# Attention and feed-forward kernel: q of five batches turned by DMA, in f16 halves, in place of TensorE transposes

## The chip, the core and the metric

The kernel runs on one core of a Trainium2 chip. The metric is the device time in microseconds. Before the change the median of three runs is 868.02 us (866.51 to 870.14).

A core has a matrix engine (TensorE, PE in the profile, its weight loads PEld), three elementwise engines (VectorE or DVE, ScalarE or ACT, GpSimd or POOL) and a queue engine (SyncE, SP) that here only starts DMAs. Each runs its own instruction queue in order and waits on semaphores for the others.

## The reference

Linear attention with 8 batches, 8 heads, 576 positions and 64 features a head, then a feed-forward layer over all 4608 tokens:

```python
q_s = softmax(q, axis=features);  k_s = softmax(k, axis=positions)
kv  = einsum('bhsd,bhse->bhde', k_s, v)          # one 64 x 64 matrix a head
x   = einsum('bhsd,bhde->bhse', q_s, kv)         # to [4608, 512]
h   = x @ w_in                                   # 512 -> 2048
out = (h * erf(softplus(h))) @ w_out             # 2048 -> 512
```

All inputs and the output are f32.

## The kernel before, in words

**Numbers.** Most f32 products are made from f16 halves: a value a is split into hi = f16(a) and lo = f16(a - hi), and a product is three f16 products (hi hi, hi lo, lo hi). A split is a copy on ACT and a subtraction on DVE. Only batches 0 and 1 and the first block of the feed-forward layer stay in f32 (`E32 = 2`).

**Feed-forward.** The tokens of two batches (a pair, 1152 tokens) are three blocks of 384. A block goes through four groups of 512 hidden features, so the kernel has 48 steps n. In step n PE makes the first product of step n in four parts m n.0 to m n.3 (function `mm1`, L905, with seven half-size products in place of eight, in product banks X, Y and Z, which ACT and DVE empty at L917 to L932), and the second product of step n - 2 in three parts M.0 to M.2 (`mm2`, L1029). Between them lie softplus and erf on ACT (L337), the multiplication (L984) and the split (L997, L1001) on DVE. Each bank of X, Y, Z exists once: PE refills it only when its last content is copied out.

**Attention.** `attention(b)` makes x for one batch. It is a generator; its stages are worked in between the parts of the feed-forward steps. A share is written for each stage (`SHARES`), and after each part of the second product `pace` takes stages until their summed shares reach the goal for that point in the program. The stages of a batch are: maximum of k over positions (`k_max`); q minus its maximum (`q_sub`); exponentials; first kv products, first half of q normalized (`q_norm`, L454 to L460); second kv products, loads of the next k and v; the kv matrix normalized and split (`kv_norm`, `kv_split`, L588, L589); second half of q normalized, and in odd batches the tail of both batches of the pair. Half means four heads over the first 512 positions; a tail is the last 64 positions of a batch, and the tails of two batches share one tile.

Then x is made for four blocks c of two heads each: PE transposes four 128x128 squares of q (`q_cols`, L610) into a bank, ACT and DVE split the bank into two f16 halves (`q_evac`, L603, L604), and, a stage later, three f16 products with kv give x (`x_mm`, L625), which ACT copies out (L436). In odd batches the tail comes ahead of the four blocks (transposes L684, the same evacuation, products into the tile xt). Behind the transposes of the second and fourth blocks stand the loads of the next batch's q (`load_q`), four DMAs each on SP.

**Order.** What the code issues is placed on each engine's queue by data and priority when the program is built; an instruction can stand earlier than its place in the code when its inputs are there early. The queues then run in that order. SP's queue carries the loads of q, k and v and the stores of results.

**Buffers.** The tiles tagged `qT` rotate over two places of 512 columns: kmax, k2, kvf and the evacuated q. The tile `raw`, 2048 f32 columns, takes raw weights and one decoded weight block at the start, which is read for the last time in step 6.

Of the kernel before, what the change touches and what calls it, by code (L numbers as in the profile page):

```python
# [8 lines left out]
F16 = mybir.dt.float16  # L9
# [44 lines left out]
def attn_moe_kernel(  # L54
# [29 lines left out]
    ch = ctx.enter_context(tc.tile_pool(name="ch", bufs=1))  # L84
    at = ctx.enter_context(tc.tile_pool(name="at", bufs=2))
    xp = ctx.enter_context(tc.tile_pool(name="xp", bufs=2))
    rp = ctx.enter_context(tc.tile_pool(name="rp", bufs=1))
    psh = ctx.enter_context(tc.tile_pool(name="psh", bufs=1, space=PSUM))
    pso = ctx.enter_context(tc.tile_pool(name="pso", bufs=1, space=PSUM))
    psa = ctx.enter_context(tc.tile_pool(name="psa", bufs=2, space=PSUM))  # L90
# [6 lines left out]
    vbuf = cp.tile([P, 4, TM, D + 1], F32, name="vbuf")  # L97
    nc.gpsimd.memset(vbuf[:, :, :, D:], 1.0)
    vtail = cp.tile([P, H, D + 1], F32, name="vtail")

    kvbd = []
    for i in range(2):
# [51 lines left out]
    def wload():  # L154


        i = nxt[0]
        while i < NPC * NJ and slots:
            w = slots.pop(0)
            if i >= NPC * (NJ - 1 if w is None else NJ if w < 2 else w - 2):  # L160
                continue
            if w == -1:
                w, other = None, "x7"
            else:
                other = None
            which, g = wjobs[i // NPC]
            a = i % NPC
            if which == "in":
                src = w_in[a * 2 * P:(a + 1) * 2 * P, 2 * g * 512:2 * (g + 1) * 512]
            else:  # L170
                src = w_out[(4 * g + 2 * a) * P:(4 * g + 2 * a + 2) * P, :]
            if other:

                raws[i] = xp.tile([P, 2, 1024], I32, tag=other, name=f"raw_{i}")
            elif w is None:
                raws[i] = rp.tile([P, 2, 1024], I32, tag="raw", bufs=1, name=f"raw_{i}")
            else:
                raws[i] = WT[w][:, :4096].bitcast(I32).rearrange("p (a n) -> p a n", a=2)
            held[i] = -1 if other else w

            eng = nc.sync if i < LOADS.count("w") else nc.gpsimd
            eng.dma_start(raws[i], src.rearrange("(a p) n -> p a n", p=P))
            nxt[0] += 1
            return

    def wdecode(i, part=None):


        jn, a = divmod(i, NPC)
        if jn not in stg:  # L190
            if jn + 2 < NJ:
                stg[jn] = WT[jn + 2][:, :4096].bitcast(F32)
            elif jn == NJ - 2:
                stg[jn] = xp.tile([P, 2048], F32, tag="x7", name=f"sg_{jn}")
            else:
                stg[jn] = rp.tile([P, 2048], F32, tag="raw", bufs=1, name=f"sg_{jn}")
        d = stg[jn][:, a * 1024:(a + 1) * 1024].bitcast(I32)
        if part is None:
            r = raws[i].rearrange("p a n -> p (a n)").rearrange("p (n two) -> p n two", two=2)
        else:  # L200
            r = raws[i][:, :, 512 * part:512 * part + 512].rearrange(
                "p a (n two) -> p a n two", two=2
            )
            d = d.rearrange("p (a n) -> p a n", a=2)[:, :, 256 * part:256 * part + 256]
        lo, hi = r[..., 0], r[..., 1]
        nc.vector.tensor_scalar(
            d, hi, 5, 2, op0=ALU.logical_shift_left, op1=ALU.logical_shift_right,
        )
        nc.vector.scalar_tensor_tensor(
            d, lo, 29, d, op0=ALU.logical_shift_right, op1=ALU.bitwise_or  # L210
        )
        nc.vector.scalar_tensor_tensor(
            d, hi, -(2**30), d, op0=ALU.bitwise_and, op1=ALU.bitwise_or
        )
        if part == 0:
            return
        raws.pop(i)
        h = held.pop(i)
        if h != -1:
            slots.append(h)  # L220
        wload()
# [262 lines left out]

    def k_max(b, ks, kt):

        kmax = at.tile([P, H, D], F32, tag="qT", name=f"kmax_{b}")
        k2 = at.tile([P, 2, 4, D], F32, tag="qT", name=f"k2_{b}")
        for hf in range(2):
            nc.vector.tensor_tensor(k2, ks[hf][:, 0:2], ks[hf][:, 2:4], op=ALU.max)  # L490
            nc.vector.tensor_tensor(
                kmax[:, hf * 4:hf * 4 + 4, :], k2[:, 0], k2[:, 1], op=ALU.max
            )
        nc.vector.tensor_tensor(kmax[kt[1]], kmax[kt[1]], kt[0], op=ALU.max)
        return kmax
# [44 lines left out]

    E32 = 2
    kv32 = [t.rearrange("p h c e -> p (h c e)").bitcast(F32) for t in kvbd]
    kv32 = [t.rearrange("p (c e) -> p c e", c=NC4) for t in kv32]

    def kv_norm(b, hf, bk):
        if b >= E32:
            if hf == 0:
                bat[b]["kvf"] = at.tile([P, NC4, D], F32, tag="qT", name=f"kvf_{b}")  # L550
            kvf = bat[b]["kvf"]
        bkv = bk[:, :2 * W].rearrange("p (c w) -> p c w", c=2)
        rd = at.tile([P, 2, 1], F32, tag="rd", bufs=1, name=f"rd_{b}_{hf}")
        nc.vector.tensor_scalar_add(rd, bkv[:, :, D:], 1e-9)
        nc.vector.reciprocal(rd, rd)
        cs = slice(2 * hf, 2 * hf + 2)
        if b >= E32:
            nc.vector.tensor_tensor(
                kvf[:, cs, :], bkv[:, :, :D], rd.to_broadcast([P, 2, D]), op=ALU.mult
            )  # L560
            return
        for a in range(2):
            ps = slice(a * D, (a + 1) * D)
            nc.vector.tensor_tensor(
                kv32[b][ps, cs, ps], bkv[ps, :, :D], rd[ps].to_broadcast([D, 2, D]),
                op=ALU.mult,
            )
# [25 lines left out]
        if b > 1:  # L593
            nc.vector.tensor_scalar_mul(d["U"], w_u["in"], d["ux"])

    def q_evac(b, bk, name):

        if b < E32:
            qT = at.tile([P, SM], F32, tag="qT", name=name)
            nc.scalar.copy(qT, bk)  # L600
            return qT[:, None, :]
        qT = at.tile([P, 2, SM], F16, tag="qT", name=name)
        nc.scalar.copy(qT[:, 0], bk)  # L603
        nc.vector.tensor_tensor(qT[:, 1], bk, qT[:, 0], op=ALU.subtract)  # L604
        return qT
# [8 lines left out]

    def q_T(b, c, bk):
        q_cols(b, c, bk)
        return q_evac(b, bk, f"qTs_{b}_{c}")

    def x_mm(b, c, out_, qT):

# [15 lines left out]
    def attention(b):  # L636
# [26 lines left out]
        d["v"].append(load_half(v, "v", b, 1))  # L663
        q_norm(rows(qs[0]), 16, f"q_{b}_0", b)
        yield SHARES[5]
        kv_norm(b, 1, kv_mm(b, 1))
        if b + 1 < B:
            load_kv(b + 1)
# [2 lines left out]
        kv_split(b, mx)  # L671
        yield SHARES[7]
        q_norm(rows(qs[1]), 16, f"q_{b}_1", b)
        if j == 1:
            q_norm(even["qt"], H, f"qt_{p}", b)
        yield SHARES[8]
        for i in ((3 * p + 1, 3 * p + 2) if j else (3 * p, 3 * p + 1)):
            while not x_free(i):
                yield 0
        if j == 1:  # L680
            qt2 = hd(even["qt"])
            bk = bank(f"qTt_{p}")
            for c in range(NC4):
                nc.tensor.transpose(  # L684
                    bk[:, c * P:(c + 1) * P], qt2[:, c * P:(c + 1) * P], ident
                )
            qT = q_evac(b, bk, f"qTt_{p}")
            if b + 1 < B:
                even_next = bat[b + 1]
                even_next["qt"] = load_tail(q, "qt", p + 1)  # L690
            yield SHARES[9]
            bk = bank(f"xt_{p}")
            x = xblock(p * NBK + 1)
            bk3 = bk.rearrange("p (c s) -> p c s", c=NC4)
            for a in range(2):
                for c in range(NC4):
                    cs = slice(c * P + a * TAIL, c * P + (a + 1) * TAIL)
                    x_mm(2 * p + a, c, bk[:, cs], qT[:, :, cs])
            for a in range(2 if b < E32 else 1):
                w = TAIL if b < E32 else P  # L700
                o = SM - T + a * TAIL
                x_put(
                    bk3[:, :, a * TAIL:a * TAIL + w], x[:, :, o:o + w],
                    bat[a]["sx"] if b < E32 else None,
                )
            yield SHARES[10]
        for c in range(NC4):
            hf, c2 = divmod(c, 2)
            qT = q_T(b, c, bank(f"qT_{b}_{c}"))
            if c2 == 1 and b + 1 < B:  # L710
                load_q(b + 1, hf)
            yield SHARES[11]
            bk = bank(f"x_{b}_{c}")
            x_mm(b, c, bk, qT)
            x_split(b, c, bk)
            if c == NC4 - 1:
                d["xdone"] = True
            yield SHARES[12]
# [14 lines left out]
    def start():  # L733
# [61 lines left out]
        def tc_(c):  # L795
# [3 lines left out]
            if c < 3:  # L799
                bk = psh.tile([P, 512], F32, tag=f"p{'XYZ'[c]}", name=f"qT_0_{c}")  # L800
                qT = r["qT"][:, c]
            else:
                bk = pso.tile([P, 512], F32, tag="o2", name=f"qT_0_{c}")
                qT = at.tile([P, SM], F32, tag="qT", name=f"qTs_0_{c}")
            q_cols(0, c, bk)
            nc.scalar.copy(qT, bk)
            put(f"t{c}", qT[:, None, :])
# [373 lines left out]
```

## Time and profile before

| what | before |
|---|---|
| runs, median (lowest, highest) | 868.02 us (866.51, 870.14) |
| profiled execution: span | 865.1 us |
| profiled execution: its own time beside the span | not listed apart; the three runs are the times there are |
| PE, busy | 823.4 us, 95% |
| DVE, busy | 642.5 us, 74% |
| ACT, busy | 505.9 us, 58% |
| POOL, busy | 18.2 us, 2% |
| mean granted TensorE clock | 0.988 |

The span runs from the first to the last instruction of one execution; the runs are other executions. A row of a group names line, engine, operation, output and inputs, shape and count, then the busy time together and the mean of one in ns, then the engine's idle time just before these instructions and what ended it. The mean of a PE matmul overlaps its neighbours. A row of the timeline or of the chain has start and length in us, then engine, line and operation; x4 stands for four in a row. "SPq" is SP's queue issuing a DMA.

### The profile page before, as it was taken

What the parts mean: (1) busy time and instruction counts of PE and PEld (TensorE: products, weight loads), DVE (VectorE), ACT (ScalarE), POOL (GpSimd) and SP (SyncE); (2) the same over time, 40 slices, a digit from 0 to 9 for tenths busy, and PEclk for the clock granted to TensorE, in tenths of its full rate; (3) what the DMA queues carried; (4) which work ended last, traced back from release to release, by engine and by line L of the source; (5) the groups of instructions that cost most, each with busy time, mean ns of one, the idle gap of its engine ahead of it and who ended that gap; (6) DMA issues with size and microseconds to landing.
All of it is one profiled execution on the core that took longest, in us unless ns stands there. A gap on an engine that the chain in (4) does not pass through costs nothing.

```text
span 865.1 us, 15558 instructions
## 1 busy us (share of the span) xinstructions
PE 823.4 (95%) x6556; PEld 570.3 (66%) x6556; DVE 642.5 (74%) x923; ACT 505.9 (58%) x646; POOL 18.2 (2%) x37
## 2 busy tenths in 40 slices
PE   3999996889999999999999999999999999999997
PEld 2655555557766677767776677776776677677672
DVE  6999799899887778858866778867865656653543
ACT  2697677576584567466655467466655456453532
POOL 2101100000000000000000000000000000000000
PEclk9999998889999999999999999999999999999999
DMA  9976730041223202311141212311010000000100
GB/s 270 402 166 184 187 86 1 1 104 26 61 50 80 65 23 50 80 38 25 33 103 32 56 30 50 80 38 25 20 43 2 24 15 1 37 2 1 37 2 37
DMA packets 117381, 55.53 MB, mean 64 GB/s; under 512 B 106560, under 2 KB 108608, under 8 KB 117312
## 3 DMA queue, kind: packets, MB, share of 16 engines
q1 hardware_dynamic: 115136, 46.15, 20.3%
q0 software_dynamic: 2176, 8.39, 2.7%
q8 instruction: 51, 0.84, 0.4%
q14 instruction: 18, 0.15, 0.0%
HBM read 45.09 MB, written 9.44 MB: 63 GB/s over the span
## 4 chain that ended last, share of the span: by engine, by line
PE 73%; DVE 13%; ACT 6%; SPq 3%; DMA 2%; issue 2%; POOL 0%; ACTq 0%; DVEq 0%
PE o L1029 33%; PE pX L905 17%; PE pZ L905 8%; PE pY L905 4%; PE kv L535 3%; ACT L337 2%; ACT G L337 2%; SPq L402 2%; DVE wt L290 2%; PE o L1020 2%; DVE G L984 2%; PE x L625 2%; PE qT L610 1%; DVE H L1001 1%; DMA q<-in_q_dram 1%
## 5 line engine op out<-in xcount | busy, mean ns | idle before, releaser
L1029 PE MATMUL o<-wt,H 128*128 128x512 f16 x1584 | 366.9, 380 | 3.6 <-DVE H L997 3.1
L905 PEld LDWEIGHTS <-wt 128*128 128x128 f16 x3696 | 312.4, 99 | 37.5 <-issue 15.2
L1029 PEld LDWEIGHTS <-H 128*128 128x128 f16 x1584 | 152.4, 98 | 159.0 <-DVE H L997 4.1
L905 PE MATMUL pX<-x,wt 128*128 128x192 f16 x2112 | 208.0, 249 | 9.8 <-ACT H L924 5.7
L337 ACT ACT_TABLE_LOAD x105 | 134.7, 1283 | 7.9 <-DVE H L930 5.7
L984 DVE SCALAR_TENSOR_TENSOR G<-G,small,H 128x1536 f32<-128x1536 f32 x44 | 80.0, 1817 | 65.9 <-ACT G L337 65.8
L905 PE MATMUL pZ<-x,wt 128*128 128x192 f16 x1056 | 103.4, 247 | 0.0
L932 ACT COPY H<-pX 128x384 f32<-128x384 f32 x44 | 20.9, 476 | 139.7 <-PE pX L905 134.7
L337 ACT ACTIVATE G<-H,U 128x768 f32<-128x768 f32 (+1 forms) x60 | 72.8, 1231 | 22.1 <-DVE H L930 21.5
L1001 DVE TENSOR_TENSOR H<-G,H 128x1536 f16<-128x1536 f32 x44 | 77.3, 1756 | 1.1
L337 ACT ACTIVATE G<-G 128x1536 f32<-128x1536 f32 x48 | 71.2, 1484 | 0.5
L905 PE MATMUL pY<-x,wt 128*128 128x192 f16 x528 | 51.1, 246 | 0.5 <-DVE H L917 0.5
L436 ACT ACTIVATE x<-x 128x384 f32<-128x384 f32 (+1 forms) x52 | 17.6, 386 | 56.4 <-PE x L625 54.0
L917 DVE COPY H<-pY 128x384 f32<-128x384 f32 x44 | 24.4, 555 | 30.1 <-PE pY L905 30.1
L997 DVE CAST H<-G 128x1536 f16<-128x1536 f32 x44 | 42.0, 955 | 0.7
L290 DVE SCALAR_TENSOR_TENSOR x<-x,x 128x768 f16<-128x768 f32 (+1 forms) x44 | 37.2, 850 | 5.7 <-ACT x L289 5.6
L289 ACT ACTIVATE x<-x 128x768 f16<-128x768 f32 (+1 forms) x44 | 33.1, 762 | 12.2 <-DVE x L381 12.1
L1045 DVE TENSOR_SCALAR ob<-o,V 128x512 f32<-128x512 f32 x29 | 21.7, 749 | 23.9 <-PE o L1029 23.7
L930 DVE TENSOR_TENSOR H<-pZ,H 128x384 f32<-128x384 f32 x44 | 24.2, 551 | 19.3 <-PE pZ L905 19.3
L919 DVE TENSOR_TENSOR H<-pX,H 128x384 f32<-128x384 f32 x44 | 24.4, 555 | 15.3 <-PE pX L905 14.9
L535 PE MATMUL kv<-vbuf,k 128*64 128x65 f32 x480 | 22.0, 237 | 7.6 <-ACT k L337 5.2
L535 PEld LDWEIGHTS kv<-vbuf,k 128*64 128x64 f32 x480 | 18.7, 149 | 14.5 <-ACT k L337 6.4
(162 smaller groups left out, 823.1 us busy)
## 6 DMA issues: line engine op xcount, KB each, us to landing
out_dram<-ob SPq DMA_DIRECT2D x32, 256.0 KB, 2.2
vbuf<-in_v_dram SPq DMA_DIRECT2D x60, 128.0 KB, 3.0
q<-in_q_dram SPq DMA_DIRECT2D x56, 128.0 KB, 3.0
k<-in_k_dram SPq DMA_DIRECT2D x56, 128.0 KB, 3.3
wt<-in_moe_w_out_dram POOLq DMA_DIRECT2D x5, 1024.0 KB, 6.5
wt<-in_moe_w_in_dram SPq DMA_DIRECT2D x4, 1024.0 KB, 10.7
raw<-in_moe_w_in_dram SPq DMA_DIRECT2D x2, 1024.0 KB, 14.3
wt<-in_moe_w_out_dram SPq DMA_DIRECT2D x2, 1024.0 KB, 16.0
```

The costliest lines, as they stand in the source:

```text
L289: nc.scalar.activation(hi, src, AF.Copy, scale=s)
L290: nc.vector.scalar_tensor_tensor(lo, src, s, hi, op0=ALU.mult, op1=ALU.subtract)
L337: i = nc.scalar.activation(out_, in_, func, **kw)
L535: nc.tensor.matmul(bk[a * D:(a + 1) * D, c * W:(c + 1) * W], kk, vv, start=(t == 0), stop=(t == TM),)
L905: nc.tensor.matmul(o, w[wl][:, c, a * P:(a + 1) * P], x[:, xl, xi, c, :], start=(new and a == 0 and c == 0 and i == 0), stop=(c == 1 and i ...
L917: nc.vector.tensor_copy(C[0, 0], bank2("Y"))
L919: add(C[0, 0], bank2("X"), C[0, 0], op=ALU.add)
L930: add(C[0, 1], bank2("Z"), C[0, 1], op=ALU.add)
L984: nc.vector.scalar_tensor_tensor(flat(s["G"]), flat(s["G"]), GA[:, g:g + 1], flat(s["H"]), op0=ALU.mult, op1=ALU.mult,)
L997: nc.vector.tensor_copy(flat(s["gh"]), flat(s["G"]))
L1001: nc.vector.tensor_tensor(flat(s["gl"]), flat(s["G"]), flat(s["gh"]), op=ALU.subtract)
L1029: nc.tensor.matmul(o, s[gt][:, a, ts_], w[wl][:, a, :], start=(first_ and a == 0 and i == 0), stop=(last_ and a == FG - 1 and i == 2),)
```

## The change

From batch 3 on (`QDMA = 3`) q isn't transposed by PE. After a half of q is normalized, `q_turn` splits it in its rows, 1024 columns at once: ACT copies it to f16, DVE subtracts, and both halves lie side by side in a scratch place. A transposing DMA on SP then reads the scratch and writes every 128x128 square, turned, over the bytes of the q tile itself, which the f32 values no longer need. The x products read it from there. The tail of odd batches goes the same way. There are three scratch places: the two halves of the tile `rw`, which was the tile `raw`, and one half of a new fixed tile `asc`, which also takes the place of the two rotating `qT` buffers for kmax, k2, kvf and the q of batches 1 and 2.

The four x blocks keep their shares. In batches 3, 5 and 7 the tail moves from ahead of the four blocks to between the second and the third. The loads of the next q move from behind the transposes to behind the products of the second and fourth blocks, since the q tile now holds the turned data; the load of the next tail moves behind the tail's products, in all odd batches.

```diff
+    asc = cp.tile([P, 2, 512], F32, name="asc")
+    rw = cp.tile([P, 2048], F32, name="rw")
...
-        kmax = at.tile([P, H, D], F32, tag="qT", name=f"kmax_{b}")
-        k2 = at.tile([P, 2, 4, D], F32, tag="qT", name=f"k2_{b}")
+        kmax = asc[:, 0].rearrange("p (h d) -> p h d", h=H)
+        k2 = asc[:, 1].rearrange("p (t h d) -> p t h d", t=2, h=4)
...
-                bat[b]["kvf"] = at.tile([P, NC4, D], F32, tag="qT", name=f"kvf_{b}")
+                bat[b]["kvf"] = asc[:, 0, :NC4 * D].rearrange("p (c e) -> p c e", c=NC4)
...
+    def q_turn(q_, hl):
+        n = hl.shape[-1] // 2
+        nc.scalar.copy(hl[:, :n], q_)
+        nc.vector.tensor_tensor(hl[:, n:], q_, hl[:, :n], op=ALU.subtract)
+        t = q_.bitcast(F16).rearrange("p (n s) -> p n s", s=P)
+        nc.sync.dma_start_transpose(t, hl)
+        return t
+
+    def q_turn_half(b, hf):
+        t = q_turn(
+            bat[b]["q"][hf].rearrange("p t h d -> p (t h d)"),
+            rw[:, 1024 * hf:1024 * hf + 1024].bitcast(F16),
+        )
+        t = t.rearrange("p (i t c) s -> p i c t s", i=2, t=TM)
+        for c in range(2):
+            bat[b].setdefault("qT", {})[2 * hf + c] = t[:, :, c]
+
+    def q_turn_tail(p):
+        t = q_turn(hd(bat[2 * p]["qt"]), asc[:, 0].bitcast(F16))
+        bat[2 * p]["qtT"] = t.rearrange("p (i c) s -> p i (c s)", i=2)
...
         q_norm(rows(qs[0]), 16, f"q_{b}_0", b)
         yield SHARES[5]
+        if b >= QDMA:
+            q_turn_half(b, 0)
         kv_norm(b, 1, kv_mm(b, 1))
...
         q_norm(rows(qs[1]), 16, f"q_{b}_1", b)
+        if b >= QDMA:
+            q_turn_half(b, 1)
         if j == 1:
             q_norm(even["qt"], H, f"qt_{p}", b)
+            if b >= QDMA:
+                q_turn_tail(p)
         yield SHARES[8]
...
+        if j == 1 and b < QDMA:
+            yield from tails()
         for c in range(NC4):
             hf, c2 = divmod(c, 2)
-            qT = q_T(b, c, bank(f"qT_{b}_{c}"))
-            if c2 == 1 and b + 1 < B:
+            if c == 2 and j == 1 and b >= QDMA:
+                yield from tails()
+            qT = q_T(b, c, bank(f"qT_{b}_{c}")) if b < QDMA else d["qT"][c]
+            if b < QDMA and c2 == 1 and b + 1 < B:
                 load_q(b + 1, hf)
             yield SHARES[11]
             bk = bank(f"x_{b}_{c}")
             x_mm(b, c, bk, qT)
+            if b >= QDMA and c2 == 1 and b + 1 < B:
+                load_q(b + 1, hf)
             x_split(b, c, bk)
```

`tails` holds the stage of the tail's transposes (now for batch 1 alone) and the stage of its products, as they were.

More of the change, by code (lines that the diff above doesn't have):

```diff
@@ L86, in attn_moe_kernel @@
     xp = ctx.enter_context(tc.tile_pool(name="xp", bufs=2))
-    rp = ctx.enter_context(tc.tile_pool(name="rp", bufs=1))
     psh = ctx.enter_context(tc.tile_pool(name="psh", bufs=1, space=PSUM))
@@ L175, in wload @@
             elif w is None:
-                raws[i] = rp.tile([P, 2, 1024], I32, tag="raw", bufs=1, name=f"raw_{i}")
+                raws[i] = rw.bitcast(I32).rearrange("p (a n) -> p a n", a=2)
             else:
@@ L195, in wdecode @@
             else:
-                stg[jn] = rp.tile([P, 2048], F32, tag="raw", bufs=1, name=f"sg_{jn}")
+                stg[jn] = rw
         d = stg[jn][:, a * 1024:(a + 1) * 1024].bitcast(I32)
@@ L539, in kv_mm @@
         return bk
-    E32 = 2
+    E32, QDMA = 2, 3
     kv32 = [t.rearrange("p h c e -> p (h c e)").bitcast(F32) for t in kvbd]
@@ L594, in kv_split, with q_evac @@
             nc.vector.tensor_scalar_mul(d["U"], w_u["in"], d["ux"])
-    def q_evac(b, bk, name):
+    def q_turn(q_, hl):
[16 more added lines that the diff above has]
+        bat[2 * p]["qtT"] = t.rearrange("p (i c) s -> p i (c s)", i=2)
+    def q_evac(b, i, bk):
         if b < E32:
[L599 to L602, printed above, removed]
+            nc.scalar.copy(asc[:, i], bk)
+            return asc[:, None, i]
+        qT = asc[:, i].bitcast(F16).rearrange("p (i s) -> p i s", i=2)
         nc.scalar.copy(qT[:, 0], bk)
@@ L616, in q_T @@
         q_cols(b, c, bk)
-        return q_evac(b, bk, f"qTs_{b}_{c}")
+        return q_evac(b, c % 2, bk)
     def x_mm(b, c, out_, qT):
@@ L679, in attention, with tails @@
                 yield 0
[L680 to L690, printed above, removed]
+        def tails():
+            if b < QDMA:
+                bk = bank(f"qTt_{p}")
+                for c in range(NC4):
+                    nc.tensor.transpose(
+                        bk[:, c * P:(c + 1) * P], hd(even["qt"])[:, c * P:(c + 1) * P], ident
+                    )
+                even["qtT"] = q_evac(b, 0, bk)
             yield SHARES[9]
+            qT = even["qtT"]
             bk = bank(f"xt_{p}")
@@ L705, in attention @@
                 )
+            if b + 1 < B:
+                bat[b + 1]["qt"] = load_tail(q, "qt", p + 1)
             yield SHARES[10]
+        if j == 1 and b < QDMA:
+            yield from tails()
         for c in range(NC4):
             hf, c2 = divmod(c, 2)
-            qT = q_T(b, c, bank(f"qT_{b}_{c}"))
-            if c2 == 1 and b + 1 < B:
+            if c == 2 and j == 1 and b >= QDMA:
+                yield from tails()
+            qT = q_T(b, c, bank(f"qT_{b}_{c}")) if b < QDMA else d["qT"][c]
+            if b < QDMA and c2 == 1 and b + 1 < B:
                 load_q(b + 1, hf)
@@ L803, in tc_ @@
                 bk = pso.tile([P, 512], F32, tag="o2", name=f"qT_0_{c}")
-                qT = at.tile([P, SM], F32, tag="qT", name=f"qTs_0_{c}")
+                qT = asc[:, 0]
             q_cols(0, c, bk)
```

## The prediction

> **What bounds the kernel now.** I read the page's first and fourth parts first (busy time, chain that ended last), then the busy time by stretch, then the chain in the stretch where attention for the last batch ends, then the groups by line.
>
> ```profile
> span 865.1 us, 15558 instructions
> ...
> PE 823.4 (95%) x6556; PEld 570.3 (66%) x6556; DVE 642.5 (74%) x923; ACT 505.9 (58%) x646; POOL 18.2 (2%) x37
> ...
> PE 73%; DVE 13%; ACT 6%; SPq 3%; DMA 2%; issue 2%; POOL 0%; ACTq 0%; DVEq 0%
> ```
>
> The chain is TensorE's for 73% of the span. Where the change acts (batches 3 to 7) it is nearly all TensorE's, as the busy time of two stretches shows (columns: busy us of PE, PEld, DVE, ACT, POOL; granted clock; DMA share; GB/s):
>
> ```profile
> 240.00:280.00 40.00, 37.45 (x372) 26.86 (x371) 32.50 (x54) 24.36 (x28) 0.64 (x2) 1.00 0.32 70
> ...
> 280.00:700.00 420.00, 417.81 (x3633) 299.18 (x3631) 311.67 (x454) 244.22 (x303) 1.89 (x6) 1.00 0.17 43
> ```
>
> From 280 to 700 us PE is idle for 2.19 us out of 420, at full clock, with 108 us free on DVE and 176 us on ACT. So each microsecond of PE work that goes away there should come off the end, unless a new wait takes its place. The 2.19 us have a place. This is the chain where batch 7's tail is transposed:
>
> ```profile
> 656.00 0.48 DVE kvbd L589
> 656.49 0.03 issue
> 656.52 0.70 DVE qTt L604
> 657.22 0.04 issue
> 657.26 0.83 PE xt L625 x23
> 658.10 1.73 PE o L1029 x8
> 659.82 0.44 PE qT L610 x4
> 660.26 0.99 PE pZ L905 x12
> ```
>
> PE is held until L604, late on a busy DVE, has split the transposed tail; then the queue runs on. Four transposes of one q block hold PE for 0.44 us, after which the next product starts at once.
>
> **The change part by part.** The rows of the operations removed, and of the nearest ones to those added:
>
> ```profile
> L610 PE MATMUL qT<-ident,q 128*128 128x128 f32 x128 | 20.0, 283 | 0.0
> ...
> L684 PE MATMUL qTt<-ident,qt 128*128 128x128 f32 x16 | 2.4, 273 | 0.0
> ...
> L625 PE MATMUL xt<-qTt,kvbd 128*128 128x64 f16 x72 | 3.1, 192 | 3.4 <-DVE qTt L604 2.1 <-ACT qTt L603 1.3
> ...
> L604 DVE TENSOR_TENSOR qTs<-qT,qTs 128x512 f16<-128x512 f32 x24 | 16.5, 686 | 9.1 <-ACT qTs L603 9.1
> L603 ACT CAST qTs<-qT 128x512 f16<-128x512 f32 x24 | 14.1, 588 | 19.1 <-PE qT L610 19.1
> L448 DVE TENSOR_TENSOR q<-q,q_m 128x1024 f32<-128x1024 f32 x14 | 17.0, 1218 | 0.1
> L337 ACT ACTIVATE q<-q 128x1024 f32<-128x1024 f32 x14 | 14.2, 1048 | 0.4 <-DVE q L448 0.3
> ```
>
> *PE transposes removed.* L610 issues 16 per batch (128 over 8 batches); five batches lose 80, in 20 groups of four. L684 issues 4 per pair; pairs 1 to 3 lose 12, in 3 groups. Each instruction's mean of 273 to 283 ns overlaps its neighbours, so I count a group by how far the next product is pushed: 0.44 us in the chain above, and for the tail the step between these two starts, 0.43 us:
>
> ```profile
> 653.57 0.60 PE L684 MATMUL qTt<-ident,qt 128*128 128x128 f32 x4
> 654.00 0.82 PE L905 MATMUL pX<-x,wt 128*128 128x192 f16 x8
> ```
>
> 23 groups by 0.44 us are 10.1 us, all on the path.
>
> *The tail's wait.* The xt products stood 3.4 us on PE, over the three tails (2.1 behind DVE, 1.3 behind ACT). After the change they come between the second and third q block and read data split and turned before. Bounds: 0 (another wait takes the place, since the same softplus, erf and DVE work stands in the step) to 3.4. I take 3.4: what is next in PE's queue, L1029, ran on without a wait behind xt.
>
> *Evacuations.* Removed: 23 splits of 512 columns, 23 x 0.686 = 15.8 us on DVE and 23 x 0.588 = 13.5 us on ACT. Added: 10 splits of 1024 columns, SBUF to SBUF, at 1.22 us (L448) and 1.05 us (the exponential of q, L337), and 3 tails at the old price: 14.3 us on DVE, 12.3 us on ACT. Both engines get about a microsecond back, which is worth nothing, as neither bounds. What can cost is their place: the ACT copy waits for DVE's normalization, DVE's subtraction waits for the copy, and behind an ACT copy stand the copies that empty product bank X. Their margin can be small:
>
> ```profile
> 636.37 0.48 ACT L924 COPY H<-pX 128x384 f32<-128x384 f32 x1
> ...
> 637.34 1.15 PE L905 MATMUL pX<-x,wt 128*128 128x192 f16 x12
> ```
>
> L924 is done 0.49 us before PE refills X. A copy of 1.05 us squeezed in just before would hold PE 0.56 us; thirteen such, 7.3 us. The removed casts stood in the same queue 23 times and cost PE nothing that shows outside the tails. Bounds 0 to 7.3; nearer the lower, I take 1.5 us.
>
> *The transposing DMAs,* ten of 512 KB and three of 256 KB, all on SP. The trace has none, so their price is bounded by these rows:
>
> ```profile
> q1 hardware_dynamic: 115136, 46.15, 20.3%
> ...
> H_raw<-in_k_dram SPq DMA_DIRECT2D x2, 512.0 KB, 4.8
> ...
> 207.80 0.62 SPq L402
> ```
>
> Near end: 512 KB takes 4.8 us as a plain load, and an issue 0.62 us of SP. Far end: q1's packets took 865.1 x 16 x 0.203 / 115136 = 24.4 ns each. If a transpose lands in pieces of 16 two-byte elements (my assumption), a half is 16384 pieces, on 16 engines 25 us. What it may take before anything waits follows from the code and these rows (DVE's normalizations for batch 7, its key-value products, its first two x products):
>
> ```profile
> 628.67 1.22 DVE L460 TENSOR_TENSOR q<-q,q_r 128x1024 f32<-128x1024 f32 x1
> ...
> 632.81 1.22 DVE L460 TENSOR_TENSOR q<-q,q_r 128x1024 f32<-128x1024 f32 x1
> 633.96 0.69 DVE L460 TENSOR_TENSOR qt<-qt,qt_r 128x512 f32<-128x512 f32 x1
> ...
> 641.01 0.69 PE L535 MATMUL kv<-vbuf,k 128*64 128x65 f32 x16
> ...
> 666.64 0.81 PE L625 MATMUL x<-qTs,kvbd 128*128 128x512 f16 x3
> ...
> 675.88 0.81 PE L625 MATMUL x<-qTs,kvbd 128*128 128x512 f16 x3
> ```
>
> In the code the first half's turn stands just ahead of the second kv products, at 641.0 at the latest; its data is ready from 629.9 and could go earlier. Its product is due no earlier than about 659.8, where the first transposes now start, so it has some 19 us even if it starts late. The tail's product comes behind the second x product, about 676. By then both halves and the tail have to pass, 2.5 halves in 35 us: **14 us a half** is the point from which PE waits. The tail has a second condition: its split goes into the place that kvf holds until L589 reads it last (656.48), which leaves some 19 us for two short operations and 256 KB. I take 5 to 8 us a half, so the cost is nothing; the cover is the time between normalization and product.
>
> *SP's queue.* Each transpose waits on SP for DVE's subtraction, and behind it stand the k and v loads of the next batch and stores of results. Those loads are used a batch later, the result buffers are next wanted a block later. q's own loads move from behind the transposes to behind the products that read the turned data, and are used a step or more later. Nothing on the path. *Fixed places* for kmax, kvf and the early q copies replace two rotating buffers of the same size: nothing, or a few tenths in batches 1 and 2.
>
> The Trainium skill speaks against the change here: "VectorE: DVE Perf Modes", section "The three transpose paths", gives 390 ns for a 128x128 transpose on TensorE against 1309 ns by DMA, and its rules send a transpose to TensorE where PSUM will do. The trace's 0.11 us for each of four on PE is cheaper still; by the page's DMA figure, blocks one after another, a half of 16 blocks would take an estimated 21 us, beyond the point above, and the time would be that of the second rival below, some 856 + 3 x (52 - 35) = 907 us. "DMA: Bandwidth & Descriptors", "Latency and other measured facts", has 261 GB/s for such transfers, which would be 2 us a half and leaves my sum as it is. No run here shows a DMA transpose yet.
>
> **The sum.** 865.1 - 10.1 - 3.4 + 1.5 = 853.1 us of span. The profiled execution is listed with its span alone; the median of the runs, 868.0, lies 2.9 us above it (866.5 to 870.1), and I carry that over: **856.0 us**, that is 12 us or 1.4% less. Its own range is 851 to 860.
>
> **The rivals.** *First: the gain is handed to ACT and DVE.* The copy and subtraction queue at worse places than the removed casts, and X-bank copies run late: thirteen times 0.56 us as above, and the tail's wait returns in another place (3.4). 868.0 - 10.1 + 7.3 = 865; range 860 to 867. For it: 0.49 us of margin in the row above, and that each half now crosses DVE, ACT, DVE. Against: two fifths of ACT and a quarter of DVE are free in the long stretch, there are 13 such crossings for 23 before, and products come much later.
>
> *Second, on the other side: a transposing DMA takes over 14 us a half.* Then batches 3, 5 and 7, with 2.5 halves to pass, stop PE at the tail's products. At the far end of 25 us: 62 - 35 = 27 us for each, three times, 81 us; the even batches, whose first half has 19 us at least, lose up to 6 each. 856 + 81 to 93 is 937 to 949; at 20 us a half, 50 - 35 = 15 us three times, 901 us. For it: two-byte pieces, and that every turn is in one queue. Against: a 512 KB transfer took 4.8 us, DMA engines are busy 17% of that stretch.
>
> *Third: no change.* The transposes go, but PE then waits at the products instead, where it had the transposes to do: the 10.1 us return as idle time in front of L625's successors. 868 less the tail's 3.4 at most, 865 to 868. Against: PE always has other ready products in the queue, 2.19 us idle out of 420.
>
> **How the numbers follow.** Forecast 0.68; first rival 0.14; second 0.12; third 0.06. What a measurement of this kernel can tell from no change is about 0.5%, 4.3 us: faster means below 863.7. The forecast and half of the first rival are faster, 0.75; the other half and most of the third the same, 0.11; the second and a little of the others slower, 0.14. The range 849 to 868 holds the forecast, the first and the third rival, and leaves out the second.
>
> **What would show it.** Right, if L610 has 48 instructions left and L684 4, PE is busy about 10 us less over the span, the xt products show no wait on L604's successor, and the q DMAs land in under 14 us a half. If the x or xt products wait for a DMA, the second rival holds; if pX waits for L924 more than the 5.7 us of now, or the chain runs through the new copy, the first; if PE's idle time rises by what its busy time fell, the third. The forecast is wrong if the time is above 862 or the idle time of PE from 280 us on exceeds 4 us.

## The result and the profile after

| | before | after |
|---|---|---|
| runs, median (lowest to highest) | 867.88 us (866.51 to 870.14) | 855.89 us (852.79 to 857.52) |
| profiled execution: span / own time | 865.1 / not listed | 852.8 / 854.95 us |
| ratio after / before, 95% interval | | 0.9864 [0.9835, 0.9892] |

The changed kernel is 12 us faster; the forecast was 856.0 us, with a span of 853.1. The page's first and fourth parts of the changed kernel:

```profile
span 852.8 us, 15390 instructions
...
PE 812.2 (95%) x6464; PEld 557.9 (65%) x6464; DVE 640.0 (75%) x913; ACT 506.1 (59%) x636; POOL 18.1 (2%) x37
...
PE 64%; DVE 20%; ACT 6%; DMA 4%; issue 3%; SPq 2%; POOL 0%; ACTq 0%; DVEq 0%
```

PE has 11.2 us less to do, and that is nearly the gain. DVE and ACT are where they were. DVE's larger share of the chain tells nothing of a loss by itself; the chain now goes back through a late load at 290 us (below). The busy time by stretch, with the columns of the prediction:

```profile
280.00:320.00 40.00, 38.87 (x335) 27.72 (x334) 28.90 (x37) 22.77 (x29) 0.00 (x0) 1.00 0.20 54
...
280.00:700.00 420.00, 418.54 (x3661) 297.75 (x3660) 313.54 (x446) 249.54 (x298) 1.90 (x6) 1.00 0.24 55
```

PE is idle for 1.46 us from 280 to 700 us, for 2.19 before; 1.13 of it is one new wait in the first 40 us. The groups that answer to those shown of before:

```profile
L637 PE MATMUL qT<-ident,q 128*128 128x128 f32 x48 | 8.0, 300 | 0.0
...
L718 PE MATMUL qTt<-ident,qt 128*128 128x128 f32 x4 | 0.6, 272 | 0.0
...
L652 PE MATMUL xt<-qt,kvbd 128*128 128x64 f16 x72 | 2.6, 193 | 0.0
...
L606 DVE TENSOR_TENSOR rw<-q,rw 128x1024 f16<-128x1024 f32 x10 | 12.2, 1218 | 0.5 <-ACT rw L605 0.5
...
L605 ACT CAST rw<-q 128x1024 f16<-128x1024 f32 x10 | 10.5, 1046 | 2.2 <-DVE q L465 2.2
...
L452 DVE TENSOR_REDUCE q_m<-q 128x16 f32<-128x1024 f32 x14 | 17.0, 1215 | 18.2 <-DMA q<-in_q_dram 18.1
```

80 and 12 transposes are gone, the xt products wait for nothing, the two halves of a split cost what L448 and the exponential of q had said (1.22 and 1.05 us). The last row has something new: the first operation on q stands 18.1 us on DVE for its loads, 2.4 us before. The transposing DMAs, as the list of issues and the view of their line give them (issue durations on SP in ns: least, median, most; then the time to landing in us):

```profile
q<-rw SPq DMA_TRANSPOSE x10, 4.3
qt<-asc SPq DMA_TRANSPOSE x3, 3.1
...
L608 SPq DMA_TRANSPOSE q<-rw x10: 1687/1962/2849, 257.6 to 630.6; - x10
L608 SPq DMA_TRANSPOSE qt<-asc x3: 1233/1235/1247, 272.3 to 648.9; - x3
```

A half of 512 KB lands 4.3 us after its issue, a tail of 256 KB after 3.1 (medians). What they cost is SP's time: 2 us an issue where a plain load takes about 0.6.

**A ledger that leaves out the start.** The start differs: PE's second product of block 1 begins at 155.5 us before and 160.7 after, and both are near level again by 201. This is not chance alone, since a variant of the kernel before (the second experiment) has 155.6 there and the changed kernel, profiled again, 159.8: the queues hold another order. I compare from the point where the second product of step 6 begins to the end of the span. The busy time over that stretch, first before, then after:

```profile
201.65:865.13 663.48, 652.18 (x5537) 460.98 (x5537) 460.93 (x643) 367.67 (x442) 2.53 (x8) 1.00 0.15 38
```

```profile
201.29:852.78 651.49, 641.22 (x5430) 449.09 (x5430) 458.75 (x637) 368.67 (x432) 2.53 (x8) 1.00 0.21 48
```

The stretch is 12.0 us shorter: PE works 11.0 us less, and its idle time falls from 11.3 to 10.3 us. The two do not hold quite the same work, though. Before has 107 matmuls more, and only 92 of them are transposes; the other 15 are half-size products (13 into bank Z, 2 into Y) that the changed kernel's queue holds ahead of this point, 1.2 us at 0.083 us each. From the transposes of k's maximum (kT) on, ahead of the first turn, the two differ by the 92 transposes alone. Before, then after:

```profile
237.33:865.10 627.77, 616.50 (x5266) 436.69 (x5264) 428.58 (x598) 347.78 (x413) 2.53 (x8) 1.00 0.14 37
```

```profile
236.33:852.80 616.47, 606.33 (x5174) 426.00 (x5172) 427.32 (x590) 348.11 (x404) 2.53 (x8) 1.00 0.21 48
```

From there the change takes off 11.3 us, 10.2 of PE's work and 1.1 of its idle time. About 1 us of the difference between the spans lies ahead of that point. Two profiles of the changed kernel agree on the longer stretch to 0.3 us: the second, on another chip, gave 651.25. The longer stretch is given for each experiment below, as "stretch"; among variants of the changed kernel with `QDMA = 3` its matmuls are the same, but for the idle transposes.

### The profile page after: what moved, and what is told of

Same layout as the page of the kernel before. It is cut to its first block, busy times and chain, and to the rows that moved or that the text cites. A ratio compares the mean times of both kernels' runs of the same rounds, so it can differ in the third digit from the quotient of the medians.

```text
span 852.8 us, 15390 instructions
## 1 busy us (share of the span) xinstructions
PE 812.2 (95%) x6464; PEld 557.9 (65%) x6464; DVE 640.0 (75%) x913; ACT 506.1 (59%) x636; POOL 18.1 (2%) x37
## 3 DMA queue, kind: packets, MB, share of 16 engines
q1 hardware_dynamic: 139104, 52.18, 24.9%
## 4 chain that ended last, share of the span: by engine, by line
PE 64%; DVE 20%; ACT 6%; DMA 4%; issue 3%; SPq 2%; POOL 0%; ACTq 0%; DVEq 0%
PE o L1070 31%; PE pX L946 16%; PE pZ L946 8%; PE pY L946 3%; DVE G L1025 2%; ACT G L342 2%; ACT L342 2%; DVE wt L295 2%; SPq L407 2%; PE x L652 2%; PE kv L540 2%; DVE H L1042 1%; DMA vbuf<-in_v_dram 1%; DMA wt<-in_moe_w_out_dram 1%; DVE wt L214 1%
## 5 line engine op out<-in xcount | busy, mean ns | idle before, releaser
L960 DVE TENSOR_TENSOR H<-pX,H 128x384 f32<-128x384 f32 x44 | 24.3, 553 | 13.2 <-PE pX L946 12.7
L452 DVE TENSOR_REDUCE q_m<-q 128x16 f32<-128x1024 f32 x14 | 17.0, 1215 | 18.2 <-DMA q<-in_q_dram 18.1
L968 DVE TENSOR_TENSOR H<-pX,H 128x384 f32<-128x384 f32 x44 | 24.2, 550 | 6.0 <-PE pX L946 5.9
```

The source lines that it names most:

```text
L960: add(C[0, 0], bank2("X"), C[0, 0], op=ALU.add)
L968: add(C[1, 1], bank2("X"), C[1, 1], op=ALU.add)
```

## The experiments

**Transposes put back, idle.** At the places of the old transposes PE transposes the identity into a bank that nobody empties.

```diff
+            if b >= QDMA:
+                idle = bank(f"idle_{b}_{c}")
+                for t in range(TM):
+                    nc.tensor.transpose(idle[:, t * P:(t + 1) * P], ident, ident)
             qT = q_T(b, c, bank(f"qT_{b}_{c}")) if b < QDMA else d["qT"][c]
...
+            else:
+                ... the same four for the tail
             yield SHARES[9]
```

> The changed kernel, with four transposes of the identity put back on PE at the 20 blocks and 3 tails where the old ones stood; nobody reads or evacuates them. Theory (the gain is PE time): 23 groups of 0.44 us come back, 10.1 us, so about 866 us against 856 for the changed kernel. Rival (the gain is that ACT and DVE no longer have to empty 23 banks in time): the evacuations stay away, so the time stays at 856 to 858.

```profile
199.80:861.21 661.41, 651.47 (x5522) 459.84 (x5522) 459.76 (x637) 368.92 (x432) 2.52 (x8) 1.00 0.20 47
```

863.1 us, ratio 0.9953 [0.9936, 0.9970]. The stretch is 9.92 us longer than the changed kernel's, against 10.1 forecast. DVE and ACT work as in the changed kernel, so the evacuations play no part: it is PE's time, 0.43 us for each of 23 groups. What is left of the gain is not the transposes. Counted from kT on, where this run has the 5266 matmuls of the kernel before, it is 627.77 - 626.14 = 1.63 us, all of it idle time:

```profile
235.06:861.20 626.14, 616.59 (x5266) 436.72 (x5264) 428.32 (x590) 348.35 (x404) 2.52 (x8) 1.00 0.20 47
```

**The tail moved, in the kernel before.** Everything by PE, with the tail between the second and third block in batches 3, 5 and 7.

```diff
-        if j == 1:
+        def tails():
             qt2 = hd(even["qt"])
...
+        if j == 1 and b < 3:
+            yield from tails()
         for c in range(NC4):
             hf, c2 = divmod(c, 2)
+            if c == 2 and j == 1 and b >= 3:
+                yield from tails()
```

> The kernel before, with one part of the change alone: in batches 3, 5 and 7 the tail (PE transposes, evacuation, products) stands between the second and the third q block. Theory (the 3.4 us that the xt products waited come from the tail's place behind a busy DVE): they go, about 864.5 us against 868. Rival (the wait comes from evacuating a bank at all, wherever the tail stands): 868, with the xt products still waiting 1 us each.

```profile
L625 PE MATMUL xt<-qTt,kvbd 128*128 128x64 f16 x72 | 3.1, 193 | 0.6 <-DVE qTt L604 0.2
```

864.85 us, ratio 0.9976 [0.9965, 0.9986]; the stretch is 661.07 us, 2.41 less than before. The wait of xt falls from 3.4 to 0.6 us, with transposes, bank and evacuation all in place. So this part of the gain belongs to the tail's place, not to the DMA.

**The tail's products first again, turned by DMA.**

```diff
-        if j == 1 and b < QDMA:
+        if j == 1:
             yield from tails()
...
-            if c == 2 and j == 1 and b >= QDMA:
-                yield from tails()
```

> The changed kernel, with the tail's products back ahead of the four q blocks, still turned by DMA. Theory (the tail needs the lead that its new place gives: its scratch is free only after the kv split, then ACT 0.6, DVE 0.7 and a DMA of 3.1 to 4.9 us): PE waits about 5 us at each of three tails, some 866 to 871 us, less if other products are queued ahead. Rival (DMA turning alone took the wait away): 856.

The waits of PE by what ended them, and the place in batch 7:

```profile
PE xt L652 <- DMA qt<-asc: 3.8, 2, 1.9
```

```profile
647.85 0.99 PE L944 MATMUL pX<-x,wt 128*128 128x192 f16 x10
650.75 0.86 PE L652 MATMUL xt<-qt,kvbd 128*128 128x64 f16 x24 [1.91 <-DMA qt<-asc]
```

857.05 us, ratio 0.9880 [0.9865, 0.9895], stretch 654.57: 3.1 us longer than the changed kernel. In batches 5 and 7 PE waits 1.9 us for the tail's DMA, more than the 1.04 us it waited for DVE before. The direction is the theory's, the size less than half of its 5 us: in batch 7 the DMA lands 4.5 us behind the kv split, near what was expected, but PE has other products until 648.8 us. In batch 3 there is no such wait. Turning by DMA alone, without the new place, would have made the tail worse.

**Each transpose three times, and six times.**

```diff
-        nc.sync.dma_start_transpose(t, hl)
+        for _ in range(3):   # or 6
+            nc.sync.dma_start_transpose(t, hl)
```

> The changed kernel with every transposing DMA issued three times in a row, with the same source and destination. A half's single transpose landed 4.3 us after its issue and held SP for 2.0 to 2.8 us, so three take 8 to 13 us. Theory (the turns have up to 14 us a half before PE waits): no change, 855 to 858 us. Rival (the lead is short in the even batches or behind SP's queue): PE waits at x products, 862 us or more.

> The same with six transposes for one: 16 to 26 us a half, beyond the 14 us. Theory: batches 3, 5 and 7 have 2.5 halves in 35 us, so PE waits 5 to 30 us in each, 870 to 945 us, and the x and xt products wait for a DMA. Rival (the queue of DMAs is never waited for at all, since products are moved behind others): 856 to 860.

The repeats wait for one another's landing, so a half takes 3 x 4.4 = 13.2 and 6 x 4.5 = 27 us. Three: one run, 860.82 us, stretch 658.50, 7.0 us longer. Its waits, on PE and on DVE:

```profile
PE xt L653 <- DMA qt<-asc: 3.7, 1, 3.7
PE pX L947 <- DVE H L969: 3.6, 4, 1.9
```

```profile
DVE asc L496 <- DMA qt<-asc: 11.0, 2, 7.0
```

```profile
287.93 1.08 PE L653 MATMUL xt<-qt,kvbd 128*128 128x64 f16 x24 [3.66 <-DMA qt<-asc]
288.82 0.51 PE L947 MATMUL pX<-x,wt 128*128 128x192 f16 x2
289.12 4.08 PE L1071 MATMUL o<-wt,H 128*128 128x512 f16 x12
```

I expected no change below 14 us a half. That point came from batch 7; in batch 3 PE comes to the tail's products 13 us behind its split (284.3 and 271.1 us), and there PE waits first. The second wait isn't for turned data: the next batch's maximum of k (L496) writes the place that the tail's DMA still reads, DVE stands 11.0 us, and PE waits for a bank that DVE has yet to empty. Six: one run, 933.7 us, stretch 732.1, 80.6 us longer, inside the 870 to 945 that was expected:

```profile
PE xt L653 <- DMA qt<-asc: 22.4, 3, 7.9
PE x L653 <- DMA q<-rw: 17.0, 4, 6.3
```

So the rival was a real one; the turn was simply three to six times too quick for it.

**The lead taken away.** The turns are written where the old transposes stood.

```diff
-        if b >= QDMA:
-            q_turn_half(b, 0)
         kv_norm(b, 1, kv_mm(b, 1))
...
-        if b >= QDMA:
-            q_turn_half(b, 1)
...
+            if b >= QDMA and c2 == 0:
+                q_turn_half(b, hf)
             qT = q_T(b, c, bank(f"qT_{b}_{c}")) if b < QDMA else d["qT"][c]
...      (and the tail's turn at the head of tails)
```

> The changed kernel with the lead taken away: a half is split and turned where its first block used to be transposed (ahead of block 1 and of block 3), the tail just ahead of its products. A turn takes ACT 1.05, DVE 1.22 and a DMA of 4.3 us, 6.6 us together without waits. Theory (the lead is what hides the turn): a block's share gives some 7.8 us to its products, so PE waits up to 3 us at ten halves and up to 5 at three tails, 860 to 890 us, about 870. Rival (the lead doesn't matter): 856.

SP's queue in batch 7, in the changed kernel and then here:

```profile
624.44 7.97 SPq L608 DMA_TRANSPOSE q<-rw  x2
648.94 1.24 SPq L608 DMA_TRANSPOSE qt<-asc  x1
```

```profile
623.54 7.81 SPq L608 DMA_TRANSPOSE q<-rw  x2
647.87 1.23 SPq L608 DMA_TRANSPOSE qt<-asc  x1
```

854.33 us, ratio 0.9848 [0.9831, 0.9865], stretch 651.13: the same. My theory falls in the form in which I put it: the written lead doesn't decide. The queues are built by when the data is there, and it is there once DVE has normalized the half (620.8 us in batch 7 of the changed kernel, where ACT's copy begins at once), wherever the turn is written; in batches 3, 5 and 7 the DMAs go out within about a microsecond of where they went, and the latest, the second half of the even batches, some 7 to 8 us later (352.0 for 344.6 us). The test did not take the lead away, so what a truly late turn costs is told by the three-fold and six-fold runs alone.

**The tail's scratch elsewhere.** `asc[:, 0]` becomes `rw[:, :512]`, the place of the first half.

> The changed kernel with the tail's scratch in the place of the first half (long read by then) in place of the one that kvf and kmax use. Theory (ACT stood 9.7 us in two waits for the kv split to free that place, and DVE 1.6 us for the tail's DMA, both beside the path): the waits go, the time is the same within 1 us, 855 to 856. Rival (these waits delay the copies that free product banks): 2 us or more faster.

853.38 us, ratio 0.9840 [0.9819, 0.9861], stretch 651.61, 0.1 us from the changed kernel. ACT's 9.7 us and DVE's 1.5 us of waiting at that place are gone, ACT stands 6.1 us at another place instead, and PE gains nothing by it.

**Batch 2 as well.** `QDMA = 2`; alone, then with the tail's scratch in `rw`, then with the turns written late too. The changed kernel ran beside the last two.

> The changed kernel with batch 2 turned by DMA as well (from batch 2 on in place of 3). Theory (PE time on the path): four more groups of 0.44 us go, 1.8 us, some 854 us. Rival (around batch 2 the chain runs through DVE and the q loads, which come later by the change): 856 to 859, with more time of DVE in wait for q.

> The changed kernel once more, beside the next two on one chip: 0.986 of the kernel before, as measured.

> Batch 2 turned by DMA too, and the tail's scratch in the place of the first half. Theory (PE time counts, the tail's scratch is beside the path): as batch 2 alone, 3 us of span below the changed kernel, within 0.5 us. Rival (the shared place with kvf and kmax costs): 1 us or more below batch 2 alone.

> The same with the turns written where the first block's transposes stood (batches 2 to 7). Since the turns ran almost as early on the queues when they were written late, theory: the same as the run before within 0.5 us. Rival (a lead written in the code puts turns ahead of more urgent work on ACT and DVE): 1 us or more faster.

| kernel | us | ratio to before, 95% interval | stretch |
|---|---|---|---|
| changed kernel, again | 853.18 | 0.9839 [0.9824, 0.9853] | 651.25 |
| batch 2 too | 851.47 | 0.9818 [0.9804, 0.9833] | 648.34 |
| and the tail's scratch in rw | 851.04 | 0.9819 [0.9804, 0.9834] | 647.72 |
| and the turns written late | 854.66 | 0.9856 [0.9839, 0.9872] | 651.70 |

Batch 2 brings 2.9 us of stretch against the changed kernel's repeat, 1.8 of it by estimate four groups of transposes; PE's wait at 290 us (below) is gone as well. Its interval still overlaps that of the changed kernel's repeat; the stretch, which repeats to 0.3 us, sets them apart. The tail's scratch is worth 0.6 us more, near the limit of what can be told. The late turns, harmless in the changed kernel, cost 4.0 us of stretch here. PE waits up to 2.6 us, at the start of batch 3,

```profile
PE pX L944 <- DVE H L966: 3.3, 3, 2.6
```

for a bank whose emptying was queued on DVE behind the subtractions from k (L675, L680), and the matmuls behind that wait run slower (last section). From kT on PE is idle 1.4 us more than in the run above it in the table and busy 1.7 us more with the same 5174 matmuls; the other 0.9 us lie ahead of kT. Both theories for this run were wrong. The order of the queues changed as a whole; which part of the new order put L966 there was not separated.

## Why the prediction was right, step by step

**PE bounds the stretch, so its work comes off one for one.** Right. The idle transposes show it alone: 10.1 us forecast, 9.92 measured. From kT on PE's busy time fell by 10.2 us; the 11.0 of the longer stretch hold the 15 products that only one side has.

**The tail's wait, 3.4 us.** Right: xt waits 0.0 us, and the kernel before with the tail moved gains 2.4 us without any DMA. I had named the tail's new place together with data turned earlier as the cause. The place is what did it; by DMA at the old place it was 1.9 us twice.

**New waits, 1.5 us.** The size was near, 2.3 us (from kT on idle time fell by 1.1 where 3.4 went), but the cause was another. The thin margin at L924 held: PE waits 0.17 us twice for an ACT copy of that kind. The largest new wait is this one, in the chain of the changed kernel:

```profile
283.67 5.54 DMA q<-in_q_dram
289.20 0.03 issue
289.23 0.05 DVEq L452
...
290.46 0.56 DVE H L960
291.02 0.04 issue
291.06 0.99 PE pX L946 x10
```

The next q is loaded behind the second block's products, lands at 289.2, and DVE, whose queue holds the first operation on q ahead of the copy that empties bank X, stands 3.4 us; PE waits 1.13 us for X (0.56 in the changed kernel's repeat). These four loads went out no later than before (281.7 us, 284.7 before), but they landed 5.3 us after their issue, in the median, where the same four took 3.0. The two loads of the next tail, which went out at 272.9 us before, now go out right behind them, at 284.4. With the tail's products first they go out at 274.3, q's loads take 3.0 us and this wait of PE is not there; since q's loads go out later there too, at 286.8, the crowding fits but is not shown alone. The step that failed is "Nothing on the path" for the moved loads: I counted when the data is used in the code, and neither where the operation that uses it was placed in DVE's queue nor what else loads at that time. In all, DVE's wait for q grew from 2.4 to 18.1 us, and only this once did PE pay.

**The transposing DMA, 5 to 8 us a half.** It took 4.3 us in the median, less than the plain load of the same size (4.8). The far end of 25 us was far off: the packets of the page rose by 139104 - 115136 = 23968 for 11.5 halves' worth, some 2084 a half, so the pieces are of some 250 B, not 32. The Trainium skill's 1309 ns for a block of 128x128 by DMA ("VectorE: DVE Perf Modes", "The three transpose paths") would have made it an estimated 21 us if blocks went one after another. Here 16 blocks land in 4.3 us, 0.27 us each, so the figure can't be added up over the blocks of one DMA; a single block was not run. The other figure, 261 GB/s ("DMA: Bandwidth & Descriptors", "Latency and other measured facts"), comes nearer: the second 256 KB of a half cost 4.3 - 3.1 = 1.2 us, by estimate 218 GB/s, on top of 3.1 - 1.2 = 1.9 us for a transpose of no size, an extrapolation from two sizes.

**14 us a half as the point from which PE waits.** Too high: 13.2 us already cost 7.0 us of stretch. It was read from batch 7 alone, and it left out the next user of the tail's scratch.

**SP's queue.** No wait of PE was traced to an issue, as forecast; an issue took 2.0 us, three times the row that I had as its near end.

**The marks set beforehand.** One was badly set: I called the forecast wrong if PE idles over 4 us from 280 us on, but the end of the kernel alone, after 835 us, has over 6 us in both profiles. The stretch from 280 to 700, which I had read, has 1.46.

**The sum.** The forecast of 12.0 us is met to 0.1 us by the medians, and that is in part luck. Where all its terms act, from kT on, the change takes off 11.3 us: 10.2 of work and 3.4 of the tail's wait, less 2.3 of new waits. The rest lies ahead of batch 3, for which the forecast had "nothing, or a few tenths in batches 1 and 2". The run with idle transposes is 3.7 us below the kernel before on its chip (866.78), 1.63 of it from kT on, and the changed kernel's repeat is 13.6 us below (866.79 to 853.18), so some 1 to 2 us come from the start; which part of its other order brings them was not separated. The 2.9 us put on the span were too many as well: the four runs of the changed kernel lie 2.1 to 2.2 us above theirs.

The other rivals: the gain was not handed to ACT and DVE (their busy time is within 2.5 us of before, and in the stretch PE's waits for a copy out of bank X went from 1.0 to 2.4 us, 1.1 of it the wait above), and PE did not wait where the transposes had been.

## What to carry to other kernels

Where one engine is busy for 99% of a stretch, work taken off it comes off the end one for one, and the measure of a group is the step it puts between its neighbours, not its instructions' mean durations. When a buffer is turned in place, ask what the later release does to the next load, and look at the consumer's place in its engine's queue, because what stands behind it there waits too, and at the other loads that then go out with it. A lead written in the code is only a lead if the built queues keep it; read the time between a DMA's landing and its first reader from the trace.

## What the runs showed of the hardware

A wait of PE costs more than its length once it passes about two microseconds. After the wait of 3.66 us with three transposes for one, twelve matmuls that take 2.75 us took 4.08, and over these 5 us the profile has a granted clock of 0.66:

```profile
288.00:293.00 5.00, 5.00 (x38) 2.66 (x38) 2.60 (x5) 3.93 (x4) 0.00 (x0) 0.66 0.67 148
```

PE's busy time in the stretch grew by 1.9 us for the same products. With six transposes, where single waits reach 7.9 us, it grew by 24.8 us of the 80.6. With batch 2 turned too and the turns written late, the same clock follows a shorter wait:

```profile
248.05 0.24 PE L944 MATMUL pX<-x,wt 128*128 128x192 f16 x1 [2.57 <-DVE H L966]
```

```profile
248.00:253.00 5.00, 4.95 (x62) 4.17 (x62) 1.92 (x4) 3.54 (x6) 0.00 (x0) 0.66 0.25 56
```

Waits of 1.13 to 1.91 us in the other runs left the clock at 1.00. The Trainium skill has this rule ("TensorE: Matmul & The Clock Gate", "Part 1: The HAM clock gate"): after an idle window of about 3.4 us the array runs at half rate until it has been busy for as long. The trace agrees in how long it lasts: 0.66 over 5 us is, at half rate, an estimated 3.4 us. It differs in what brings it: 2.57 us did here, 1.91 did not. The price of my second rival left it out.
